# Attention backward loop: every dS unit transposed by DMA, none by TensorE

## The chip, the cores and the metric

The kernel runs on one core of a Trainium2 chip. The metric is the device time of one execution in microseconds (us); lower is better. The kernel before takes 2543.87 us in the median of three runs (2539.78 to 2545.97). Its profile is of one further execution, whose span from the first to the last instruction is 2533.7 us.

## What is computed

The reference is one transformer block with adaptive layer norm, and the gradient of all its inputs. What matters here is attention, `x` of 2048 tokens by 512, 32 heads of 16 columns each, and its backward pass through `jax.vjp`:

```python
qkv = (x @ wqkv).reshape(B, S, 3, H, Dh)          # H = 32 heads, Dh = 16
scores = jnp.einsum('bhqd,bhkd->bhqk', q, k) * Dh ** (-0.5)
p = _softmax(scores, axis=-1)
o = jnp.einsum('bhqk,bhkd->bhqd', p, v)
...
_out, _vjp = jax.vjp(_f, A_x, A_wqkv, A_wo, B_w1, B_b1, B_w2, B_b2, c, w_mod)
_grads = _vjp(grad_out)
```

For each head the backward pass rebuilds the probabilities E = exp(scale * q k), forms dP from the output gradient and v, and multiplies them to dS. Then dK sums dS over queries, dV sums E over queries, and dQ sums dS over keys. dK and dV can take dS and E with queries on the partitions, as they are made; dQ needs dS with keys on the partitions, that is, transposed. All outputs (the block's output and nine gradients) are bf16.

## The kernel before

The kernel is one program with stages: projections and the forward attention (to about 1000 us of the profile), the dense layers and their gradients interleaved with it, the attention backward loop (about 1123 to 2408 us), and a last stage that turns dQ, dK and dV into the gradients of the input and the weights. The change lies in the backward loop alone.

**Units and blocks.** The loop runs over 512 units: 8 head groups of 4 heads, 4 key chunks of 512 keys, 4 query chunks, 4 query tiles of 128 queries. A unit holds 128 queries by 4 heads by 512 keys: 128 partitions of 2048 bf16 elements, 512 KB. Four units with the same head group, key chunk and query chunk form a block; there are 128 blocks.

**What is done for a unit.**

- `score` (line 1595): four TensorE matmuls, one a head, each into one PSUM bank of 128x512. The banks A, B and C are taken in an order that a string gives (`bank`). Bank C has the tag `px`.
- `expo` (line 1601): four ScalarE exponentials from those banks into the SBUF tile `E_u` (4 buffers).
- `dp_pair` (lines 1613 and 1615): for each pair of heads two TensorE matmuls into a PSUM tile `psD_u`, and one VectorE multiplication with `E_u` into the SBUF tile `dS_u` (6 buffers). So a unit has two VectorE instructions.
- `k_quad` and `v_quad` (lines 1650 and 1659): four TensorE matmuls each, summed in the PSUM tile `accVK` over the 16 query tiles, and copied out by ScalarE (line 1662).
- `transpose_unit` (line 1628): the SP queue issues one DMA transpose of the whole `dS_u` into a quarter of the block's tile `dsT` (3 buffers, one a block).

**What is done for a block.** `dq_quad` (line 1677) makes 16 TensorE matmuls from `dsT` into the PSUM tile `dqacc`, also under the tag `px`; `dq_out` (lines 1687, 1690 and 1695) copies it with ScalarE and adds it up on GpSimd.

**The fourth unit of every odd block** is treated otherwise: `transpose_unit` returns without a DMA, and `pe_turn` (line 1640) makes 16 TensorE transposes of 128x128 in two halves, each into a PSUM tile under the tag `px`; ScalarE copies each half into `dsT` (line 1756, 128x1024 elements). That is one unit in eight: 448 units go by DMA, 64 by TensorE. Around the two halves `keep_warm` (line 1633) adds matmuls with a zero weight tile to `accVK`, which change no value; the token f places them.

**What sets the order.** TensorE, ScalarE, VectorE, SP and GpSimd run in the written order in this stage. The order is two token strings: s is a score, e an exponential, D a `dp_pair` (and after every second one the unit's transpose), q a `k_quad` or `v_quad`, t and T a half of `pe_turn` and its ScalarE copy, f a `keep_warm`, d half of a block's `dq_quad`, and Q its `dq_out`. `order_t` serves the passes whose preceding block is odd, `order_n` the others. D runs about one unit behind e, and a pass that issues the scores of block b issues the `dq_quad`s of block b-2:

```python
order_t = ("s0 s1 q s2 e0 e1 D s3 D e2 s4 e3 t1 e4 q T1 D "
    "s5 s6 e5 f f t2 e6 s7 T2 e7 D s8 e8 D f f s9 e9 q q s10 "
    "s11 e10 D d1 d2 e11 Q q s12 D e12 s13 e13 q s14 D e14 "
    "s15 q q e15 ").split(), "ABCABBABACABABCA"
order_n = ("s0 D s1 q e0 q s2 e1 e2 D s3 s4 q s5 e3 D e4 "
    "e5 s6 q s7 D s8 e6 e7 d1 e8 s9 D d2 e9 q Q s10 "
    "s11 e10 D q s12 e11 e12 s13 e13 D q s14 s15 e14 e15 D q ").split(), "CBACBACBABABCABC"
```

**Other transfers in the loop.** ScalarE's queue issues the loads of the next head group and the stores of dK, dV and dQ (lines 1577 and 1667, 1699), from a list of due times in units. SP issues, besides the transposes, five loads for the last stage in the last head group (line 1547) and the last stage's loads after the last transposes (lines 1775 and on).

Of the kernel before, what the change touches and what calls it, by code (L numbers as in the profile page):

```python
# [14 lines left out]
AF = mybir.ActivationFunctionType  # L15
ALU = mybir.AluOpType
AX = mybir.AxisListType
BF = dt.bfloat16
F32 = dt.float32

P = 128
D = 512
# [12 lines left out]
def kernel(  # L35
# [17 lines left out]
    PE = nc.tensor  # L53
    DVE = nc.vector
    ACT = nc.scalar
# [6 lines left out]
    identb = persist.tile([P, P], BF, name="identb")  # L62
# [84 lines left out]
    with ExitStack() as ph:  # L147
# [1053 lines left out]
        def head_fill(i):  # L1201
            for key in ("k", "v", "q", "do"):
                POOL.memset(hsets[i][key][:], 1.0 if key in ("k", "v") else 0.0)
# [345 lines left out]
    with ExitStack() as ph:  # L1549
# [4 lines left out]
        psx = ph.enter_context(tc.tile_pool(name="psIx", bufs=1, space=bass.MemoryType.PSUM))  # L1554
        units = [(hg, kc, qc, qi) for hg in range(HG) for kc in range(QC) for qc in range(QC) for qi in range(4)]
        NU = len(units)
        hst, bst, sst, dqt, cur = {}, {}, {}, {}, {}

        def load_head(hg):
            st = dict(hsets[hg % 2])  # L1560
            st["qz"] = qz[hg % 2]
            st["acc"] = stg.tile([P, n], F32, name="dQacc", tag="dQacc", bufs=1)
            st["dq"] = stg.tile([P, n], BF, name="dQst", tag="dQst", bufs=1)
            st["vk"] = stg.tile([P, n], BF, name="vkb", tag="vkb")
            hst[hg] = st
# [22 lines left out]
        def score(u, hq, bank):  # L1588
            hg, kc, qc, qi = units[u]
            st = hst[hg]  # L1590
            qt = qc * 4 + qi
            r = 32 * hq
            psS = psx.tile([P, 512], F32, name=f"psS_{bank}", tag=banks[bank])
            sst[u, hq] = psS
            PE.matmul(psS[:], st["q"][r:r + 32, qt * P:(qt + 1) * P], st["k"][r:r + 32, kc * 512:kc * 512 + 512],  # L1595
                      start=True, stop=True, tile_position=(r, 0))

        def expo(u, hq):
            if hq == 0:
                bst[u] = [ework.tile([P, 4, 512], BF, name="E_u", tag="E_u"), None]  # L1600
            ACT.activation(bst[u][0][:, hq, :], sst.pop((u, hq))[:], AF.Exp, scale=SCALE)  # L1601

        def dp_pair(u, pair):
            hg, kc, qc, qi = units[u]
            st = hst[hg]
            qt = qc * 4 + qi
            if pair == 0:
                bst[u][1] = ework.tile([P, 4, 512], BF, name="dS_u", tag="dS_u", bufs=6)
            E_u, dS_u = bst[u]
            psD = psd.tile([P, 2, 512], F32, name="psD_u", tag="pd")  # L1610
            for hi in range(2):
                r = 32 * (2 * pair + hi)
                PE.matmul(psD[:, hi, :], st["do"][r:r + 32, qt * P:(qt + 1) * P], st["v"][r:r + 32, kc * 512:kc * 512 + 512],  # L1613
                          start=True, stop=True, tile_position=(r, 0))
            DVE.tensor_tensor(dS_u[:, 2 * pair:2 * pair + 2, :], psD[:], E_u[:, 2 * pair:2 * pair + 2, :], ALU.mult)  # L1615
            if qi == 3 and on_pe(u // 4):
                held["dS"] = dS_u

        def on_pe(b):
            return b % 2 == 1  # L1620

        def transpose_unit(u):
            hg, kc, qc, qi = units[u]
            if qi == 0:
                dqt[u // 4] = tpool.tile([P, 4, 16, P], BF, name="dsT", tag="dsT")
            if qi == 3 and on_pe(u // 4):
                return
            SP.dma_start(out=dqt[u // 4][:, qi], in_=bst[u][1].rearrange("p h k -> p (h k)"), transpose=True)

        held = {}  # L1630

        def keep_warm():
            PE.matmul(cur["vk"][0:DH, :], KS_tok[:, 0, D:QPAD], dOs_tok[:, 0, :], start=False, stop=False,
                      tile_position=(0, 0), skip_group_check=True)

        def pe_turn(b, half):
            pt = psx.tile([P, 8, P], BF, name="ptT", tag="px")
            for i in range(8):
                kt = i % 4
                PE.transpose(pt[:, i, :], held["dS"][:, 2 * half + i // 4, kt * P:(kt + 1) * P], identb[:])  # L1640
            dst = dqt[b][:, 3, 8 * half:8 * half + 8, :]
            held[half] = (dst, pt)

        def k_quad(u):
            hg, kc, qc, qi = units[u]
# [34 lines left out]
        def dq_out(b):  # L1680
# [17 lines left out]
                    r = hg % 2 * 64 + hq * DH  # L1698
                    at(cur["j"] + 6 + hq, load, dQc[hg // 2, r:r + DH, :], st["dq"][32 * hq:32 * hq + DH, :])

        order_t = (
            "s0 s1 q s2 e0 e1 D s3 D e2 s4 e3 t1 e4 q T1 D "
            "s5 s6 e5 f f t2 e6 s7 T2 e7 D s8 e8 D f f s9 e9 q q s10 "
            "s11 e10 D d1 d2 e11 Q q s12 D e12 s13 e13 q s14 D e14 "
            "s15 q q e15 ").split(), "ABCABBABACABABCA"
        order_n = (
            "s0 D s1 q e0 q s2 e1 e2 D s3 s4 q s5 e3 D e4 "
            "e5 s6 q s7 D s8 e6 e7 d1 e8 s9 D d2 e9 q Q s10 "
            "s11 e10 D q s12 e11 e12 s13 e13 D q s14 s15 e14 e15 D q ").split(), "CBACBACBABABCABC"
# [6 lines left out]
        with tc.manual_schedule(engines={PE.engine, ACT.engine, DVE.engine, SP.engine, POOL.engine}):  # L1716
            head_fill(1)
            POOL.memset(qz[1][:], 0.0)
            nD, nq = -1, -4
            idle = psx.tile([P, 512], F32, name="idle", tag="accVK")  # L1720
            for b in range(NU // 4 + 3):
                toks, bank = order_t if on_pe(b - 1) else order_n
                for tok in toks:
                    c, i = tok[0], int(tok[1:] or 0)
                    if c == "s" and b < NU // 4:
                        if i == 0 and units[4 * b][1:] == (0, 2, 0) and units[4 * b][0] + 1 < HG:
                            load_head(units[4 * b][0] + 1)
                        score(4 * b + i // 4, i % 4, bank[i])
                    elif c == "e" and b < NU // 4:
                        expo(4 * b + i // 4, i % 4)  # L1730
                        if b < 2 and i % 2 == 1:
                            if nq > 0:
                                keep_warm()
                            elif nq < 0:
                                PE.matmul(idle[:], ones_bf[:], identb.unsqueeze(1).to_broadcast([P, 4, P]), start=True, stop=True)
                    elif c == "D":
                        if 0 <= nD < 2 * NU:
                            dp_pair(nD // 2, nD % 2)
                            if nD % 2 == 1:
                                transpose_unit(nD // 2)  # L1740
                        nD += 1
                        cur["j"] = nD
                        for j in sorted(j for j in todo if j <= nD):
                            for f, args in todo.pop(j):
                                f(*args)
                    elif c == "q":
                        if 0 <= nq < 2 * NU:
                            (v_quad if nq % 2 else k_quad)(nq // 2)
                        nq += 1
                    elif c == "f" and 0 < nq < 2 * NU:  # L1750
                        keep_warm()
                    elif c == "t" and 0 <= b - 1 < NU // 4:
                        pe_turn(b - 1, i - 1)
                    elif c == "T" and 0 <= b - 1 < NU // 4:
                        dst, pt = held.pop(i - 1)
                        ACT.activation(dst, pt[:], AF.Identity)  # L1756
                    elif c == "d" and 0 <= b - 2 < NU // 4:
                        for kt in (2 * i - 2, 2 * i - 1):
                            dq_quad(b - 2, kt)
                    elif c == "Q" and 0 <= b - 2 < NU // 4:  # L1760
                        dq_out(b - 2)
            assert not todo
        dq_last = hst[HG - 1]["dq"]

    with ExitStack() as ph:
# [15 lines left out]
        order = (("vk", 6), ("vk", 0), ("vk", 1), ("vk", 2), ("vk", 3), ("dq", 0), ("vk", 7), ("dq", 1), ("vk", 4), ("dq", 2), ("vk", 5), ("dq", 3))  # L1781
# [140 lines left out]
        with tc.manual_schedule(engines={PE.engine, ACT.engine, DVE.engine}):  # L1922
            for k, (key, i) in enumerate(order):
                for g in range(2):
                    if (2 * k + g) % 2 == 0:
                        pt = pst.tile([P, 8, P], BF, name="ptq", tag="ptq")
                    else:
                        pt = psd.tile([P, 8, P], BF, name="ptd", tag="pdh1")
                    for ti in range(8):
                        t = 8 * g + ti  # L1930
                        PE.transpose(pt[:, ti, :], xs[key, i][:, t * P:(t + 1) * P], identb[:])
                    if key == "dq":
                        dst = dq_tok[:, 8 * g:8 * g + 8, i * P:(i + 1) * P]
                    else:
                        dst = dvk_tok[:, 8 * g:8 * g + 8, i, :]
# [32 lines left out]
            for b in range(3):  # L1968
                for ic in range(DC):
                    dwqkv(b, ic)  # L1970
                    i = b * DC + ic
# [75 lines left out]
```

## Time and profile before

| | |
|---|---|
| Time, median of 3 runs | 2543.87 us (2539.78 to 2545.97) |
| Span of the profiled execution | 2533.7 us; its own time is not recorded apart from the span. The median of the runs is 10.2 us above it |
| Backward loop, first DMA transpose issued to the SP queue's last one done issuing | 1126.15 to 2405.17 us: 1279.0 us |
| Busy, whole span | TensorE 93%, ScalarE 91%, VectorE 71%, GpSimd 14% |
| Busy, 1400 to 1600 us | TensorE 192.85, VectorE 190.54, ScalarE 197.18 of 200 us |
| Mean granted TensorE clock | 0.978 of full speed |

How to read what follows: a row of a group of instructions gives source line, engine, operation, output and inputs, shapes and count, then the busy time in us and the mean of one in ns, then the idle time of the engine just before these instructions and what ended it. SPq is the SP engine's DMA queue: its rows are the issuing instructions, and their duration is the time for which the queue was held by one, not the transfer itself. A view of the DMA queues gives the packets and bytes that each queue moved in a stretch, and the share of the 16 DMA engines that they took; the share can pass 100%, because packets of one engine overlap in the records.

### The profile page before, as it was taken

To read this page: it belongs to the slowest core of one execution; us is meant where nothing else is said; L and a number is where in the kernel's file an instruction comes from. 1 tells how busy PE (TensorE), PEld (TensorE's weight loads), DVE (VectorE), ACT (ScalarE), POOL (GpSimd) and SP (SyncE) were. 2 spreads that over 40 slices of the span, in tenths; PEclk is the share of its full clock that TensorE was granted. 3 is DMA by queue.
4 is the path that set the end of the run, shared out by engine and by line. 5 is a ranking of instruction groups with operands and counts; after the bars stand their busy time and mean duration, and the time that the engine had idled before them with its cause. 6 is when DMAs were issued, how large, how long until landed. Compare 5 with 4: busy or idle time off the path is not lost.

```text
span 2533.7 us, 50560 instructions
## 1 busy us (share of the span) xinstructions
PE 2353.2 (93%) x19005; PEld 777.5 (31%) x19005; DVE 1808.8 (71%) x2317; ACT 2305.1 (91%) x3577; POOL 348.5 (14%) x370
## 2 busy tenths in 40 slices
PE   7898889989988998999999999999999999999999
PEld 3232223223322323533232223232232322332343
DVE  5555153454444455579899999899998998998872
ACT  7999999999999999549999999999999998998952
POOL 2000001211323141110101101011010110100100
PEclk9999999999999999999899999999999999999999
DMA  6477454366649765979999999999999999999972
GB/s 204 126 191 190 140 130 128 90 164 144 94 101 193 129 144 119 276 199 194 189 201 199 198 197 203 197 195 201 206 202 195 202 195 199 202 203 207 200 241 73
DMA packets 1227131, 447.21 MB, mean 177 GB/s; under 512 B 1103096, under 2 KB 1197752, under 8 KB 1226631
## 3 DMA queue, kind: packets, MB, share of 16 engines
q1 hardware_dynamic: 1198966, 409.14, 81.9%
q0 software_dynamic: 10944, 16.78, 4.6%
q10 hardware_dynamic: 16976, 18.07, 2.6%
q8 instruction: 149, 2.44, 0.4%
q14 instruction: 96, 0.78, 0.1%
HBM read 96.75 MB, written 73.95 MB: 67 GB/s over the span
## 4 chain that ended last, share of the span: by engine, by line
PE 41%; ACT 37%; DVE 7%; issue 7%; DMA 5%; SPq 2%; ACTq 0%; POOL 0%; DVEq 0%; POOLq 0%
ACT E_u L1601 23%; ACT ET L562 11%; PE dqacc L1677 5%; PE psST L560 4%; PE psS_A L1595 3%; PE pm L233 3%; DMA dsT<-dS_u 2%; PE accVK L1650 2%; PE oacc L576 2%; PE psS_B L1595 2%; ACT dsT L1756 2%; PE pdh L1871 2%; PE psS_C L1595 2%; SPq L178 2%; PE pm L412 2%
## 5 line engine op out<-in xcount | busy, mean ns | idle before, releaser
L1615 DVE TENSOR_TENSOR dS_u<-psD_u,E_u 128x1024 bf16<-128x1024 f32 x1024 | 1186.1, 1216 | 93.0 <-PE psD_u L1613 27.2
L562 ACT ACTIVATE ET<-psST 128x1024 bf16<-128x1024 f32 x1024 | 942.7, 1240 | 23.4 <-PE psST L560 22.7
L1601 ACT ACTIVATE E_u<-psS_A 128x512 bf16<-128x512 f32 x768 | 507.8, 661 | 14.1 <-DMA out_dram<-xlast 7.2
L1601 ACT ACTIVATE E_u<-psS_B 128x512 bf16<-128x512 f32 x768 | 501.2, 653 | 8.9 <-PE psD_u L1613 2.2
L1613 PE MATMUL psD_u<-iv,ido 32*128 32x512 bf16 x2048 | 412.0, 390 | 5.4 <-DVE dS_u L1615 5.2
L560 PE MATMUL psST<-qt_sb,kt_sb 32*128 32x512 bf16 x2048 | 315.7, 387 | 50.4 <-ACT ET L562 45.5
L1601 ACT ACTIVATE E_u<-psS_C 128x512 bf16<-128x512 f32 x512 | 332.8, 650 | 13.4 <-DMA dsT<-dS_u 9.9
L1595 PE MATMUL psS_A<-ik,iq 32*128 32x512 bf16 x768 | 296.2, 386 | 11.2 <-ACT E_u L1601 1.1
L1595 PE MATMUL psS_B<-ik,iq 32*128 32x512 bf16 x768 | 297.1, 387 | 9.4 <-ACT E_u L1601 1.9
L1595 PEld LDWEIGHTS <-iq 32*128 32x128 bf16 x2048 | 130.0, 91 | 319.1 <-issue 303.4
L1650 PE MATMUL accVK<-dS_u,qz 128*32 128x512 bf16 x2048 | 215.4, 392 | 0.9 <-DVE dS_u L1615 0.6
L576 PE MATMUL oacc<-ET,vaug 128*32 128x512 bf16 x2048 | 207.4, 395 | 3.2 <-DVE ostage L580 3.2
L1659 PE MATMUL accVK<-E_u,dOs_tok 128*16 128x512 bf16 x2048 | 204.6, 388 | 0.0
L1695 POOL TENSOR_TENSOR dQacc<-dQacc,dqtmp 128x512 f32<-128x512 f32 x64 | 81.3, 1270 | 875.5 <-ACT dqtmp L1690 875.5
L1595 PE MATMUL psS_C<-ik,iq 32*128 32x512 bf16 x512 | 195.1, 381 | 4.2
L560 PEld LDWEIGHTS <-kt_sb 32*128 32x128 bf16 x2048 | 85.1, 91 | 339.6 <-issue 319.1
L1677 PE MATMUL dqacc<-dsT,KS_tok 128*32 128x512 bf16 x2048 | 150.1, 392 | 25.2 <-ACT E_u L1601 10.9
L1756 ACT ACTIVATE dsT<-ptT 128x1024 bf16<-128x1024 bf16 x128 | 144.4, 1128 | 10.1 <-PE ptT L1640 9.6
L251 DVE COPY part<-pm 128x512 f32<-128x512 f32 (+2 forms) x103 | 63.4, 616 | 117.6 <-PE pm L233 109.2
L1613 PEld LDWEIGHTS <-ido 32*128 32x128 bf16 x2048 | 105.8, 91 | 105.7 <-issue 99.5
L1650 PEld LDWEIGHTS <-qz 128*32 128x32 bf16 x2048 | 58.9, 94 | 179.2 <-issue 164.9
L576 PEld LDWEIGHTS <-vaug 128*32 128x32 bf16 x2048 | 53.0, 93 | 122.2 <-issue 122.2
(407 smaller groups left out, 2515.4 us busy)
## 6 DMA issues: line engine op xcount, KB each, us to landing
p_st<-part POOLq DMA_DIRECT2D x36, 256.0 KB, 5.2
kt_sb<-qkT_st SPq DMA_DIRECT2D x124, 64.0 KB
wA<-in_B_w_dram SPq DMA_DIRECT2D x28, 256.0 KB
dsT<-dS_u SPq DMA_TRANSPOSE x448
wB<-w1T_st SPq DMA_DIRECT2D x21, 256.0 KB
wA<-w2T_st SPq DMA_DIRECT2D x21, 256.0 KB
wB<-in_B_w_dram SPq DMA_DIRECT2D x21, 256.0 KB
p_st<-part POOLq DMA_DIRECT2D x25, 192.0 KB, 4.2
```

What stands on the lines that cost most here:

```text
L560: PE.matmul(ps[:, hi, :], kt_sb[r:r + 32, kt * P:(kt + 1) * P], qt_sb[r:r + 32, :], start=True, stop=True, tile_position=(r, 0))
L562: ACT.activation(ET[:, 2 * pair:2 * pair + 2, :], ps[:], AF.Exp, scale=SCALE)
L576: PE.matmul(oacc[32 * hq:32 * hq + 32, :], lhsT, ET[:, hq, :], start=(kt == 0), stop=(kt == TT - 1), tile_position=(0, 32 * hq), skip_grou ...
L1595: PE.matmul(psS[:], st["q"][r:r + 32, qt * P:(qt + 1) * P], st["k"][r:r + 32, kc * 512:kc * 512 + 512], start=True, stop=True, tile_positi ...
L1601: ACT.activation(bst[u][0][:, hq, :], sst.pop((u, hq))[:], AF.Exp, scale=SCALE)
L1613: PE.matmul(psD[:, hi, :], st["do"][r:r + 32, qt * P:(qt + 1) * P], st["v"][r:r + 32, kc * 512:kc * 512 + 512], start=True, stop=True, til ...
L1615: DVE.tensor_tensor(dS_u[:, 2 * pair:2 * pair + 2, :], psD[:], E_u[:, 2 * pair:2 * pair + 2, :], ALU.mult)
L1650: PE.matmul(cur["vk"][32 * hq:32 * hq + 32, :], hst[hg]["qz"][:, qt, hq, :], bst[u][1][:, hq, :], start=(qt == 0), stop=False, tile_positi ...
L1659: PE.matmul(acc[32 * hq:32 * hq + DH, :], dOs_tok[:, qt, (hg * 4 + hq) * DH:(hg * 4 + hq + 1) * DH], E_u[:, hq, :], start=False, stop=(qt ...
L1677: PE.matmul(acc[32 * hq:32 * hq + 32, :], KS_tok[:, kc * 4 + kt, h * DH:h * DH + 32], tT[:, :, hq * 4 + kt, :], start=(kt == 0), stop=(kt ...
L1695: POOL.tensor_tensor(dst2, dst, tmp[:], ALU.add)
L1756: ACT.activation(dst, pt[:], AF.Identity)
```

## The change

All 512 units go through `transpose_unit`. `on_pe`, `held`, `pe_turn`, the ScalarE copies (token T), the tokens t and f and the string `order_t` are gone; every pass runs the string `order_n` with its bank order. `keep_warm` remains in the first two passes only. The order of SP's other transfers, the pools and their buffer counts, and everything outside the loop are as they were.

```diff
             DVE.tensor_tensor(dS_u[:, 2 * pair:2 * pair + 2, :], psD[:], E_u[:, 2 * pair:2 * pair + 2, :], ALU.mult)
-            if qi == 3 and on_pe(u // 4):
-                held["dS"] = dS_u
-
-        def on_pe(b):
-            return b % 2 == 1
 
         def transpose_unit(u):
             hg, kc, qc, qi = units[u]
             if qi == 0:
                 dqt[u // 4] = tpool.tile([P, 4, 16, P], BF, name="dsT", tag="dsT")
-            if qi == 3 and on_pe(u // 4):
-                return
             SP.dma_start(out=dqt[u // 4][:, qi], in_=bst[u][1].rearrange("p h k -> p (h k)"), transpose=True)
...
-        def pe_turn(b, half):
-            pt = psx.tile([P, 8, P], BF, name="ptT", tag="px")
-            for i in range(8):
-                kt = i % 4
-                PE.transpose(pt[:, i, :], held["dS"][:, 2 * half + i // 4, kt * P:(kt + 1) * P], identb[:])
-            dst = dqt[b][:, 3, 8 * half:8 * half + 8, :]
-            held[half] = (dst, pt)
...
-        order_t = (
...
-        order_n = (
+        order = (
             "s0 D s1 q e0 q s2 e1 e2 D s3 s4 q s5 e3 D e4 "
             "e5 s6 q s7 D s8 e6 e7 d1 e8 s9 D d2 e9 q Q s10 "
             "s11 e10 D q s12 e11 e12 s13 e13 D q s14 s15 e14 e15 D q ").split(), "CBACBACBABABCABC"
...
-                toks, bank = order_t if on_pe(b - 1) else order_n
+                toks, bank = order
...
-                    elif c == "f" and 0 < nq < 2 * NU:
-                        keep_warm()
-                    elif c == "t" and 0 <= b - 1 < NU // 4:
-                        pe_turn(b - 1, i - 1)
-                    elif c == "T" and 0 <= b - 1 < NU // 4:
-                        dst, pt = held.pop(i - 1)
-                        ACT.activation(dst, pt[:], AF.Identity)
```

## The prediction

> **What bounds the kernel now.** First the page's busy shares: over the loop TensorE, ScalarE and VectorE are all above 90%, so none of them singles itself out. Then the slices of the DMA engines, where the loop begins at about slice 18:
>
> ```profile
> DMA  6477454366649765979999999999999999999972
> GB/s 204 126 191 190 140 130 128 90 164 144 94 101 193 129 144 119 276 199 194 189 201 199 198 197 203 197 195 201 206 202 195 202 195 199 202 203 207 200 241 73
> ```
>
> The reader is to see that the DMA row is at 9 through the whole loop, and that the rate there hardly moves, 189 to 207 GB/s, which is how a limit looks. A busy share alone does not prove one, so next the time-ordered rows of the SP queue, then the transposes' own row:
>
> ```profile
> 1126.15 1137.26 SPq L1628 DMA_TRANSPOSE dsT<-dS_u  x399
> 2263.46 0.99 SPq L1547 DMA_DIRECT2D iq<-dVKtP  x1
> 2264.55 9.31 SPq L1628 DMA_TRANSPOSE dsT<-dS_u  x3
> ```
>
> ```profile
> L1628 SPq DMA_TRANSPOSE dsT<-dS_u x448: 1681/2670/4379, 1126.1 to 2401.7; - x150
> ```
>
> 399 transposes are issued one behind the other, shown as one piece: 1137.26 / 399 = 2.85 us each. The shortest issue took 1.681 us, so the usual 2.67 is not what issuing must cost; the queue is held by what lies before it. The view of SP's waits between 1150 and 2430 us (total, times, longest) names another cause:
>
> ```profile
> SPq L1628 <- DVE dS_u L1615: 946.0, 439, 4.3
> ```
>
> This says VectorE, and I do not believe it, because dS is there long before. I counted both lines up to one unit (two windows, to 1709.1 and to 1701.4 us):
>
> ```profile
> L1628 SPq DMA_TRANSPOSE dsT<-dS_u x203: 1681/2682/4379, 1126.1 to 1709.0; - x102
> ...
> L1615 DVE TENSOR_TENSOR dS_u<-psD_u,E_u x462: 1210/1214/1226, 1124.9 to 1701.3; 128x1024 bf16<-128x1024 f32 x154
> ```
>
> 462 VectorE instructions are units 0 to 230. Of these 231 units 28 are the fourth of an odd block, so 203 have a DMA transpose. The last of them begins to issue at 1709.0, though its data was done at 1701.3 + 1.2 = 1702.5: 6.5 us late, two to three transposes. The queue works off a backlog. So the loop sits on two limits at once: the engines make 4 units in 1279.0 / 128 = 9.99 us, and the DMA turns 3.5 of them in that time.
>
> **What one transpose costs the DMA.** I looked for stretches in which nothing but transposes moved, and for one with other traffic (12.3, 12.0 and 21 us long, from 1281.1, 2317.9 and 1699 us):
>
> ```profile
> DMA packets 10349, 2.61 MB, mean 212 GB/s; under 512 B 10349, under 2 KB 10349, under 8 KB 10349
> ```
>
> ```profile
> DMA packets 10381, 2.62 MB, mean 218 GB/s; under 512 B 10381, under 2 KB 10381, under 8 KB 10381
> ```
>
> ```profile
> q1 hardware_dynamic: 14556, 3.67, 119.6%
> q10 hardware_dynamic: 128, 0.26, 3.9%
> ```
>
> A unit is 0.524 MB. The quiet stretches give 0.524 / 212 GB/s = 2.47 us and 2.40 us; a third, 1744.6 to 1752.2 us at 208 GB/s, gives 2.52. I take the middle, 2.47. In the third stretch above, SP's queue (q1) moved 3.67 MB, 7 units, in 21 us: 3.0 us each, while ScalarE's queue (q10) moved only 0.26 MB. So the loads of the next head cost the transposes more than their bytes. Over the loop 448 x 2.47 = 1106.6 us are bare transposes; 1279.0 - 1106.6 = 172.4 us are other transfers, what they cost the transposes, and the few gaps.
>
> **The change, part by part.**
>
> *Added: 64 DMA transposes*, on a queue that has no room. 64 x 2.47 = **+158.1 us**. The 172.4 us stay, since the other transfers are the same in number and size. The engines give nothing back: a block then needs (512 x 2.47 + 172.4) / 128 = 11.2 us of the queue, against 9.99 us that the engines need today. Bounds: from below, the other transfers might cost no more than their own share of the DMA engines in the loop (4.3% for ScalarE's queue, 0.5% for instructions and the rest, of 1279.0 us: 61 us) and some 14 us for the five or six 512 KB loads on SP; then 512 x 2.47 + 75 = 1340 us, +61. From above, each added transpose meets traffic as the present ones do: 64 x 2.85 = +182. I take +158, which is nearer to the row that counts this kernel's own transposes in bulk.
>
> *Removed: 128 ScalarE copies* (144.4 us busy, 1128 ns each) and *1024 TensorE transposes* (82.3 us busy), 255 of the 266 zero products (84.7 us busy, overlapping others). They lie on ScalarE and TensorE, which after the change wait for the queue, so they are worth 0. If the queue were faster than I think, they are worth up to what VectorE leaves: its 1024 instructions come one each 1.146 us where nothing stops them (10 in 11.46 us at 1811.66), 1174 us, and 93.0 us idle before them, so at most 93 us.
>
> *Moved: every pass uses the string of the even ones.* It ends with s15 in bank C and begins with s0 in bank C, where before the two strings alternated and the borders differed (C then A, A then C). So at each of 127 borders s0 waits for e15 (0.65 us), and ScalarE then waits for s0 (0.38 us); behind s0 on TensorE are D and the q matmuls, so VectorE waits too. 0.4 to 1.0 us a border, 50 to 130 us in all if nothing covered it. The cover is the queue's 11.2 us a block against the engines' 9.99 less the removed copies (144.4 / 128 = 1.1 us a block): some 2 us. I cost it at 0.
>
> *Moved by the backlog: where the engines stop.* Up to 6 units of dS may be held (6 buffers), and d1 in a pass needs the transposes of two blocks before, while about 6 younger units are already made. So TensorE stops at line 1677 and VectorE at line 1615 with 5 or 6 units queued, some 13 us of work: the queue does not run dry while they restart. These stops cost no more than the queue's own time, as long as the restart is shorter than that. The chain of waits (start, length, what) has such stops already:
>
> ```profile
> 1622.62 6.85 DMA dsT<-dS_u
> 1629.49 0.31 ACTq L1577
> ```
>
> After this one TensorE ran at a granted clock of 0.50 from 1630.2 to 1633.6 us, and the 16 matmuls of line 1677 took 1.90 us instead of twice 0.61. So each long stop brings 3.4 us at half speed, about 1.7 us lost, inside the 13 us of backlog.
>
> *The end of the loop.* The last transpose is now unit 511's, and the stage behind it starts from the queue's end as before: 2533.7 - 2405.2 = 128.5 us, unchanged.
>
> **Sum.** 1126.15 + 512 x 2.47 + 172.4 + 128.5 = 2691.7 us of span, 158.0 more than 2533.7. With the 10.2 us by which the median of the runs exceeds the span, **2702 us**.
>
> [...]
>
> **Rivals.**
>
> 1. *Proportional*: 2.85 us for each added transpose, 2543.9 + 182 = 2726. For it: the 399 in one piece. Against: the other transfers do not grow. It lies within my range.
> 2. *The traffic thins out*: with a queue that is never empty the other transfers hide between the transposes; +61, 2605. Against it: the queue is backlogged today, and still takes 3.0 us with traffic.
> 3. *Restarts not covered*: the stops come every block instead of now and then, each with half speed behind it and the bank border on top; if 0.5 us a block shows, 64 us more: 2766. It decides where TensorE at half speed needs longer than the backlog lasts.
> 4. *Faster*: the transposes run at the pace of the freed engines. It needs all traffic together in under 1279 / 512 = 2.50 us a unit; beyond that point the 144.4 us of copies come off ScalarE and VectorE's 93 us of idle time bound the gain. Half of it, 46 us: 2498. For it: quiet stretches do reach 2.40 to 2.52, just at the point. Against: the queue's mean is 2.85 with nothing idle between.
> 5. *No change*: the queue absorbs 64 more, and the freed engine time is lost at the bank borders: 2544. It needs both 4's condition and the border price.
>
> **Chances.** Forecast with rival 1, 2640 to 2750: 0.80. Rival 2 below 2640: 0.07. Rival 3 above 2750: 0.07. Rival 4: 0.04. Rival 5: 0.02. The range is 2640 to 2750; the low end goes towards rival 2, and the high end lies between rivals 1 and 3. A measurement of this kernel tells about 0.3%, 8 us, from no change: faster 0.04, same 0.02, slower 0.94.
>
> **What would show it.** The profile after has 512 transposes in a stretch of about 1437 us, 2.8 us each, with the DMA row at 9; ScalarE's and VectorE's busy shares in the loop fall to some 80 to 85%; lines 1677 and 1615 now wait for `dsT<-dS_u` for 100 us and more in sum; quiet stretches still show 208 to 218 GB/s. I am wrong if the transposes take under 2.5 us in the mean, if SP's queue shows gaps, or if the waits at s0 of a block carry the chain.

## The result, and the profile after

The changed kernel takes 2692.06 us (median of four runs, 2687.72 to 2694.22), the kernel before 2541.82 us in its four runs. The ratio is **1.0596, 95% interval 1.057 to 1.0621**: 150 us slower. The prediction was 2702 us with a range of 2640 to 2750. The span of the profiled execution is 2685.9 us.

The page's slices of the kernel after, in the place of those shown of before (PEclk is the granted TensorE clock in tenths):

```profile
PEclk9999999999999999878888788787886887878789
DMA  7476562468476669799999999999999999999982
GB/s 204 130 188 166 146 148 78 130 166 141 89 154 146 132 122 273 193 183 202 197 201 199 208 202 201 205 202 199 199 202 203 207 204 198 200 208 206 198 246 83
```

The DMA row is at 9 through the loop and the rate is where it was, about 200 GB/s. The loop is longer because more bytes pass at the same rate. What is new is the clock row. It was at 9 in all but one slice of before, and is now at 6 to 8.

The SP queue in order of time, and the transposes' row:

```profile
1126.23 1271.97 SPq L1621 DMA_TRANSPOSE dsT<-dS_u  x455
2398.25 0.58 SPq L1547 DMA_DIRECT2D iq<-dVKtP  x1
```

```profile
L1621 SPq DMA_TRANSPOSE dsT<-dS_u x512: 1619/2558/4433, 1126.2 to 2556.5; - x171
```

455 transposes stand in one piece of 1271.97 us, 2.80 us each (before: 399 at 2.85). One piece is no proof of a backlog, here or in the prediction, because the view merges rows of one kind across waits. A run below (e7), whose queue waits for the engines, shows its transposes as one piece too, 5.08 us each:

```profile
1133.18 1159.29 SPq L1623 DMA_TRANSPOSE dsT<-dS_u  x228
```

What tells a backlog is how long a finished dS waits, which follows below. The queue is done issuing the last one at 2558.41 us, 1432.2 us after the first (before: 1279.0). What follows takes 2685.9 - 2558.4 = 127.5 us (before: 128.5). The loop grew by 153.2 us and the span by 152.2, so all of the loss lies in the loop.

This is the same count as in the prediction, of transposes issued and VectorE instructions begun (windows from 1126 us to 1858.6 and to 1849 us). One VectorE instruction lies before the window in both kernels, so one is to be added to its count:

```profile
L1621 SPq DMA_TRANSPOSE dsT<-dS_u x261: 1619/2524/4094, 1126.2 to 1858.6; - x131
```

```profile
L1615 DVE TENSOR_TENSOR dS_u<-psD_u,E_u x521: 1214/1217/1226, 1124.9 to 1848.4; 128x1024 bf16<-128x1024 f32 x174
```

521 + 1 halves are units 0 to 260, the last done at 1848.4 + 1.2 = 1849.6 us. Its transpose, the 261st, begins to issue 9.0 us later. I left out that one instruction in the prediction, so the lag that I gave for before, 6.5 us, was 7.6. Over the whole loop a finished dS waits 3.0 us (median) for its transpose's issue before, and 6.3 us after. Only 25 of 448 transposes before and 21 of 512 after begin within 0.1 us of their data, so the queue was behind nearly all the time in both kernels.

The engines between 1400 and 2200 us, before and after (busy time of TensorE, its weight loads, VectorE, ScalarE and GpSimd, then the clock, the DMA share and GB/s):

```profile
1400.00:2200.00 800.00, 760.39 (x7260) 237.44 (x7257) 747.35 (x646) 773.51 (x1474) 91.18 (x66) 0.99 1.17 199
```

```profile
1400.00:2200.00 800.00, 688.69 (x5803) 164.81 (x5795) 679.41 (x580) 650.09 (x1250) 83.13 (x61) 0.81 1.17 203
```

VectorE fell from 93% to 85%, ScalarE from 97% to 81%; the DMA's numbers hardly moved. The waits of the loop (total, times, longest) show where the stops are:

```profile
DVE dS_u L1615 <- PE psD_u L1613: 130.4, 174, 5.4
PE psS_C L1595 <- ACT E_u L1601: 102.0, 119, 2.4
...
ACT E_u L1601 <- DMA dsT<-dS_u: 42.3, 19, 6.1
...
DVE dS_u L1615 <- DMA dsT<-dS_u: 22.3, 23, 2.1
```

The second line is the bank border (s0 waits for e15). It looks large, and whether it costs anything no wait row can say. Nor do the direct waits for the transposes account for the loss: 42.3 and 22.3, and 9.9 us at line 1660 (5.0 of its matmuls and 4.9 of their weight loads). The 42.3 us are ScalarE's, whose exponentials read no transposed data. Each of these 19 waits stands just behind a DMA issue of ScalarE's own (line 1577), which was held until one of SP's transposes had landed; ScalarE runs in the written order, so its exponentials stood still with it. A stop of one engine shows up as the other engines' waits for that one: TensorE at line 1660 waited for ScalarE 43 times, 40.9 us. In the chain that ended last, the transposes' share of the loop went from 4.8% to 11.7%.

### The profile page after: what moved, and what is told of

Same layout as the page of the kernel before. It is cut to its first block, busy times and chain, and to the rows that moved or that the text cites. A ratio compares the mean times of both kernels' runs of the same rounds, so it can differ in the third digit from the quotient of the medians.

```text
span 2685.9 us, 48010 instructions
## 1 busy us (share of the span) xinstructions
PE 2368.4 (88%) x17724; PEld 695.9 (26%) x17724; DVE 1825.4 (68%) x2317; ACT 2223.3 (83%) x3449; POOL 347.2 (13%) x370
## 4 chain that ended last, share of the span: by engine, by line
PE 50%; ACT 26%; DMA 8%; DVE 8%; issue 6%; SPq 1%; ACTq 0%; POOL 0%; DVEq 0%
ACT E_u L1601 14%; ACT ET L562 11%; DMA dsT<-dS_u 6%; PE dqacc L1660 6%; PE psS_A L1595 5%; PE psS_B L1595 4%; PE psS_C L1595 4%; PE accVK L1633 4%; PE accVK L1642 3%; PE psST L560 3%; PE pm L233 2%; PE oacc L576 2%; DVE dS_u L1615 2%; PE pdh L1842 2%; PE pwq L1876 2%
## 5 line engine op out<-in xcount | busy, mean ns | idle before, releaser
L1601 ACT ACTIVATE E_u<-psS_B 128x512 bf16<-128x512 f32 x768 | 468.5, 610 | 112.2 <-PE psD_u L1613 69.2
L1613 PE MATMUL psD_u<-iv,ido 32*128 32x512 bf16 x2048 | 467.0, 452 | 10.5 <-DVE dS_u L1615 10.2
L1601 ACT ACTIVATE E_u<-psS_C 128x512 bf16<-128x512 f32 x640 | 392.7, 614 | 98.9 <-PE psS_B L1595 59.8
L1601 ACT ACTIVATE E_u<-psS_A 128x512 bf16<-128x512 f32 x640 | 393.6, 615 | 43.2 <-PE psD_u L1613 20.1
L1595 PE MATMUL psS_B<-ik,iq 32*128 32x512 bf16 x768 | 347.0, 452 | 23.6 <-ACT E_u L1601 14.1
L1595 PE MATMUL psS_C<-ik,iq 32*128 32x512 bf16 x640 | 276.3, 432 | 103.5 <-ACT E_u L1601 102.0
L1660 PE MATMUL dqacc<-dsT,KS_tok 128*32 128x512 bf16 x2048 | 207.9, 492 | 61.7 <-ACT E_u L1601 40.9
L1633 PE MATMUL accVK<-dS_u,qz 128*32 128x512 bf16 x2048 | 245.8, 461 | 2.2 <-DVE dS_u L1615 1.7
L1642 PEld LDWEIGHTS <-dOs_tok 128*16 128x16 bf16 x2048 | 49.7, 87 | 152.0 <-issue 152.0
L1660 PEld LDWEIGHTS <-KS_tok 128*32 128x32 bf16 x2048 | 41.1, 100 | 182.1 <-issue 168.4
```

Of the source, the lines that this page charges most:

```text
L1633: PE.matmul(cur["vk"][32 * hq:32 * hq + 32, :], hst[hg]["qz"][:, qt, hq, :], bst[u][1][:, hq, :], start=(qt == 0), stop=False, tile_positi ...
L1642: PE.matmul(acc[32 * hq:32 * hq + DH, :], dOs_tok[:, qt, (hg * 4 + hq) * DH:(hg * 4 + hq + 1) * DH], E_u[:, hq, :], start=False, stop=(qt ...
L1660: PE.matmul(acc[32 * hq:32 * hq + 32, :], KS_tok[:, kc * 4 + kt, h * DH:h * DH + 32], tT[:, :, hq * 4 + kt, :], start=(kt == 0), stop=(kt ...
```

## The experiments

**Theories.** *Queue*: the SP transpose queue sets the loop's end, before nearly and after wholly. *Border*: s0 waits for e15 at 127 borders. *Clock*: TensorE at half speed, since the zero products and the turns are gone, is what is late.

The ratio is to the kernel before. The clock is that of 1400 to 2200 us, and the last column is the median time for which a finished dS waits for its transpose's issue (by the trace, unit by unit).

| Run | DMA transposes | Ratio (95%) | Clock | dS waits, us |
|---|---|---|---|---|
| before | 448 | 1 | 0.99 | 3.0 |
| after | 512 | 1.0596 (1.057 to 1.0621) | 0.81 | 6.3 |
| e1_only_add | 512 | 1.0628 (1.0585 to 1.0672) | 0.88 | 6.9 |
| e2_only_order | 448 | 1.0107 (1.0056 to 1.0158) | 0.87 | 1.6 |
| e3_other_banks | 512 | 1.0616 (1.0583 to 1.065) | 0.83 | 7.3 |
| e4_no_v_products | 512 | 1.0827 (1.079 to 1.0864) | 0.54 | 0.03 |
| e5_no_head_loads | 512 | 1.0468 (1.0438 to 1.0499) | 0.81 | 6.7 |
| e6_one_in_sixteen | 480 | 1.0322 (1.0288 to 1.0355) | 0.89 | 4.9 |
| e7_half_the_transposes | 256 | 1.0036 (1.0013 to 1.0058) | 0.87 | 0.03 |
| e8_v_for_zero | 512 | 1.0559 (1.0531 to 1.0586) | 0.81 | 6.6 |
| e9_zero_products | 512 | 1.0642 (1.0604 to 1.0679) | 0.94 | 5.2 |
| e10_half_banks_zero | 256 | 1.0212 (1.018 to 1.0243) | 1.00 | 0.03 |
| e11_half_banks | 256 | 0.9626 (0.9594 to 0.9657) | 1.00 | 0.03 |
| e12_before_no_zero | 448 | 1.0089 (1.0067 to 1.0112) | 0.94 | 2.0 |

### The 64 transposes alone, and the order alone

In the kernel before, `transpose_unit` no longer returns early, and the copies of the TensorE turns go to a tile that is not read:

```diff
-            if qi == 3 and on_pe(u // 4):
-                return
...
-            dst = dqt[b][:, 3, 8 * half:8 * half + 8, :]
+            dst = wk.tile([P, 8, P], BF, name="unread", tag="unread", bufs=2)[:]
```

> The kernel before, with both token strings, the TensorE turns, the ScalarE copies and the zero products all kept; only the 64 left-out DMA transposes are added, and ScalarE's copies go to a tile that nothing reads. Queue theory (SP's transpose queue sets the loop's end): as the changed kernel, 2685 to 2710 us, 512 transposes at 2.80 us. Clock theory (the loss comes from TensorE at half speed once the zero products and the fixed rhythm are gone): under 2600, since they are all there. Border theory (s0 waits for e15 at 127 block borders): 2545, since the old strings have no such border.

The run takes 1.0628, 2705 us. With every turn, copy and zero product still there, the added transposes bring the whole loss. The SP queue of this run:

```profile
1136.41 1281.87 SPq L1626 DMA_TRANSPOSE dsT<-dS_u  x455
```

That is 2.82 us each. The other half of the change is the changed kernel without those 64 (its three `dsT` tiles are allocated once and set to zero, so that an unwritten quarter may stay; dQ is then wrong):

```diff
+            if qi == 3 and u // 4 % 2 == 1:
+                return
             SP.dma_start(out=dqt[u // 4][:, qi], in_=bst[u][1].rearrange("p h k -> p (h k)"), transpose=True)
```

> The changed kernel without the fourth unit's transpose in odd blocks (that quarter of dsT keeps old data, so dQ is not computed rightly): 448 transposes, one token string, no TensorE turns. Queue theory: 448 x 2.47 + 172 = 1279 us of loop, 2530 to 2555. Border theory: the price of 127 borders stays, 2590 to 2670. Clock theory: 2600 and more.

The run takes 1.0107, 2570 us. Border and clock expected 2590 and more, the queue theory at most 2555; it lies between, so no theory alone met it. The order has a price of some 27 us where the queue is less loaded (a dS waits 1.6 us). The two prices do not add up: 6.28% and 1.07% apart, 5.96% together.

> The kernel before with TensorE turning the fourth unit of every fourth block only: 480 transposes by DMA, 32 units by TensorE, the old string t around those and the other string elsewhere. Queue theory: half of the 64 added transposes, so about half of the loss: 1.030 of before, 2610 to 2630. Border or clock theories: the runs above gave the order at most 1.011 by itself, so under 1.012.

In the kernel before only `on_pe` changes, from `b % 2 == 1` to `b % 4 == 1`. The run takes 1.0322, 2627 us: 448, 480 and 512 transposes give 1, 1.032 and 1.060.

### The bank border

```diff
-            "s11 e10 D q s12 e11 e12 s13 e13 D q s14 s15 e14 e15 D q ").split(), "CBACBACBABABCABC"
+            "s11 e10 D q s12 e11 e12 s13 e13 D q s14 s15 e14 e15 D q ").split(), "CBACBACBABABACBA"
```

> The changed kernel with another bank order, whose last score uses bank A and not C, so that s0 of the next block waits for nothing. Queue theory: 2692 within 8 us; the waits of bank C at line 1595 (102 us in the changed kernel) go, and come back at lines 1660 and 1615. Border theory: 40 us or more off.

The run takes 1.0616, no gain. The 102 us of TensorE at bank C are gone from the waits. TensorE's waits at the banks A and B and the waits for the transposes have grown in their place (bank B from 14.1 us, bank A from next to none):

```profile
ACT E_u L1601 <- DMA dsT<-dS_u: 57.8, 22, 5.3
DVE dS_u L1615 <- ACT E_u L1601: 50.4, 65, 4.6
...
DVE dS_u L1615 <- DMA dsT<-dS_u: 43.7, 49, 2.1
...
PE psS_B L1595 <- ACT E_u L1601: 35.8, 28, 4.7
PE psS_A L1595 <- ACT E_u L1601: 30.6, 87, 0.4
```

So a wait of 102 us in the table was worth nothing, because the queue was later. It is worth a great deal where the queue is not. The next three runs leave out the transposes of every second unit, so their dQ is wrong; the second has the banks of the diff above as well, and the third those and the string with six zero products that is shown further down:

```diff
+            if qi % 2 == 1:
+                return
```

> The changed kernel with the transposes of every second unit left out (those quarters of dsT keep old data, so dQ is not computed rightly): 256 transposes need some 256 x 2.47 + 172 = 805 us, far under the engines' pace. It shows what the engines need under the new order when the queue never holds them. If the queue alone had set the loop before and after: 2450 to 2500. If the order without turns and zero products has a price of its own, as the run with 448 transposes hints (1.0107 of before): 2550 to 2580, TensorE's clock at 0.85 to 0.9 in the loop.

> The same with the other bank order and no zero products: tells the two apart. If the border waits (98 us at line 1595 with 448 transposes) were what the order cost: below 2510, as with both. If it was TensorE's clock: near 2554, and only the zero products help.

> The run with half of the transposes, with the bank order that has no wait at the block border and six zero products a pass. With a free queue, 1.0036 of before was what the engines needed under the new order, though 144 us of ScalarE's copies were gone. If the border and the half-speed stretches took that gain: 40 us or more under before, below 2500. If the engines' pace has another bound (VectorE, 1174 us at its closest): still within 20 us of before.

With half of the transposes the new order takes 2554 us, as long as before, though 144 us of ScalarE's copies and 82 us of TensorE's turns are gone. With the other banks it takes 2449.5. The border cost 104 us, 0.8 us for each of 127. TensorE's time at half speed in the loop went with it, from 382 us to 48, so the 104 us are the border's waits and the slow clock behind them together; no run parts the two. Without the border VectorE is busy 99% of the time, and the clock stays at 1.00 without a zero product in this stretch:

```profile
1400.00:2200.00 800.00, 723.53 (x6991) 202.37 (x6988) 793.41 (x700) 780.64 (x1509) 97.61 (x72) 1.00 0.72 130
```

That is the pace of the engines with a queue that never holds them and no turns: 96 us under before. Six zero products a pass on top make it 2599.5, outside both expectations (below 2500, or within 20 us of before). 768 of them cost 150 us, 0.195 us each, since TensorE is then the late one (790.64 of 800 us busy).

### TensorE's clock

> The changed kernel without the 2048 TensorE products of E and the output gradient (line 1642), so dV is not computed. A fifth of TensorE's work in the loop is gone, and no transfer. Queue theory: 2692 within 10 us. Clock theory (TensorE, half of the time at half speed, is what is late): 50 us or more off.

The edit takes out the four matmuls in `v_quad` and lets those of `k_quad` close the sum, so dV is not computed. The run takes 1.0827, 2754 us, **some 60 us slower than after, for less work**. Neither expectation foresaw that: I had looked for no change or a gain. The row for 1400 to 2200 us:

```profile
1400.00:2200.00 800.00, 685.02 (x4387) 135.27 (x4384) 649.20 (x548) 626.90 (x1180) 77.93 (x57) 0.54 1.08 192
```

The clock is at 0.54: half speed for 1362 us of the run's loop, against 555 us after and 71 us before (from the first transpose's issue to the end of the last one's). And a finished dS waits only 0.03 us (median; 363 of 512 begin within 0.1 us), so the queue mostly waits for the engines. The DMA share is 1.08 all the same, so a DMA row at 9 does not prove a backlog either. Here the clock theory holds, and the queue theory does not. One zero product in place of each four V products:

```diff
-            for hq in range(4):
-                PE.matmul(acc[32 * hq:32 * hq + DH, :], dOs_tok[:, qt, (hg * 4 + hq) * DH:(hg * 4 + hq + 1) * DH], E_u[:, hq, :],
-                          start=False, stop=(qt == TT - 1), tile_position=(0, 32 * hq), skip_group_check=True)
+            keep_warm()
```

> The changed kernel with each four V products replaced by one zero product (line 1633's form), so dV is not computed. Without V products the loop took 1.0827 of before with the clock at 0.55 and an idle queue. If that loss was the clock, and one zero product keeps TensorE as busy as the four products side by side: back to the queue's limit, 2685 to 2710, clock 0.8. If the loss was something else that the V products did: still 2750.

The run takes 1.0559, 2690 us: back at the queue's limit, with the clock at 0.81.

```profile
1400.00:2200.00 800.00, 689.86 (x4949) 162.83 (x4941) 683.80 (x584) 653.39 (x1257) 83.09 (x61) 0.81 1.16 203
```

TensorE's busy time is hardly different between the last two rows (685 and 690 us), because its matmuls are longer at half speed (685.02 us for 4387 of them is 156 ns each, 689.86 us for 4949 is 139; a score matmul of before took 0.37 us at 1624.49 us, at a clock of 1.00, and 0.60 us at 1632.75 us, at 0.50); the busy column does not show this, the clock column does. Is the changed kernel itself held by its clock of 0.81? Its string with six zero products:

```diff
-            "s0 D s1 q e0 q s2 e1 e2 D s3 s4 q s5 e3 D e4 "
-            "e5 s6 q s7 D s8 e6 e7 d1 e8 s9 D d2 e9 q Q s10 "
-            "s11 e10 D q s12 e11 e12 s13 e13 D q s14 s15 e14 e15 D q ").split(), "CBACBACBABABCABC"
+            "s0 D s1 q f e0 q s2 e1 e2 D s3 s4 q s5 f e3 D e4 "
+            "e5 s6 q s7 D s8 f e6 e7 d1 e8 s9 D d2 e9 q Q s10 f "
+            "s11 e10 D q s12 e11 e12 s13 f e13 D q s14 s15 f e14 e15 D q ").split(), "CBACBACBABABCABC"
```

> The changed kernel with six zero products a pass put back into the string. Queue theory: the clock rises from 0.81 to 0.9 or more in the loop, and the time stays at 2692 within 10 us. If the half-speed stretches cost time of their own in the changed kernel: 20 us or more off.

The clock rises from 0.81 to 0.94, and the time to 1.0642. The faster clock bought nothing here; the time lies 12 us (by the ratios) to 17 us (by the medians) above after, a little more than the 10 that I had allowed. The zero products are work for TensorE too, so this run is not the clock alone; but a finished dS still waits 5.2 us for the queue. So after is the queue's, not the clock's.

The stop that the prediction showed left TensorE idle for 3.71 us, with a clock of 0.50 behind it. Stops of that length are too few to account for the slow clock: after has 60 half-speed stretches in the loop, and TensorE stood idle for more than 3.71 us three times; without the V products there are 40 stretches, 1362 us in all, and the longest idle time is 1.8 us. So much shorter stops went with the slow clock here. The border's are among them, as 382 us of half speed with it against 48 without show in the pair above; under the full queue the other bank order leaves 533 us of after's 555, and no run shows what the clock went with there.

### The head's loads

```diff
-            for i, (to, fro) in enumerate(loads):
+            for i, (to, fro) in enumerate(loads if hg == 1 else ()):
```

> The changed kernel, but the loads of the next head group's k, q, v, do and q rows are issued once only (heads 2 to 7 reuse what is there, so their gradients are of other heads): 126 of ScalarE's transfers in the loop are left out, about 8 of its 14.4 MB. If the loads cost the transposes more than their bytes (172.4 us for all, some 120 of it not gaps): 60 to 90 us off the changed kernel, near 2610 to 2630. If they cost only their own share of the DMA engines (61 us in all): about 35 off, 2655 to 2665. If TensorE's clock and not the queue is what is late: no gain.

132 transfers are left out (22 for each of six heads, 8.07 of 14.40 MB; the expectation says 126), and the gradients are of other heads. The run takes 1.0468, 2669 us: 23 us under after by the medians, 1.3% of before (33 us) by the ratios. The queue's longest piece:

```profile
1133.05 1243.96 SPq L1621 DMA_TRANSPOSE dsT<-dS_u  x455
```

That is 2.73 us each in place of 2.80, 28 us for 455. It is the lower of the two figures expected, about the loads' own share of the DMA engines. So these loads are a small part of what lifts the queue's mean from 2.47 to 2.80. Another part the after trace shows in one transpose (1664.06 to 1667.63 us, 40 slices of 89 ns):

```profile
DMA  9999299900000000000100003999999999999999
GB/s 267 235 166 103 40 350 272 155 0 0 0 0 0 0 0 6 6 9 9 11 6 11 11 9 66 298 284 284 301 287 284 290 298 278 295 295 281 295 295 251
...
q1 hardware_dynamic: 2082, 0.52, 127.0%
q8 instruction: 1, 0.02, 1.6%
```

One 16 KB packet of the queue that the view calls instruction (q8), in what follows an instruction fetch, begins at 1664.54 us and takes 0.93 us. The transpose stream stops for some 1.4 us, and then catches up at 290 GB/s. The transpose needed 3.57 us. So it is nearly everywhere in the loop: 76 of its 81 such packets have a pause of 1.0 us or more in the stream within 2 us of them (under 20 packets of SP's queue begin in each 0.1 us, where the mean is 74), and only 7 such pauses lie elsewhere.

The 511 times from one transpose's issue to the next part as follows. In 81 a fetch packet begins, and they last 3.40 us in the mean; 221 hold no packet of another queue and last 2.48; the other 209 hold packets of ScalarE's queue (loads and stores) or of the second instruction queue (q14) and last 2.90. Above 2.48 that is 74 us for the fetches and 88 us for the rest. No run here took the fetches away, so this is a reading and not an experiment, and it may be too high: without the 132 loads the same reading gives 48 us for the rest, 40 less, while the loop became only 25.3 us shorter (1406.9 us).

### The zero products of before

```diff
-        "s5 s6 e5 f f t2 e6 s7 T2 e7 D s8 e8 D f f s9 e9 q q s10 "
+        "s5 s6 e5 t2 e6 s7 T2 e7 D s8 e8 D s9 e9 q q s10 "
```

> The kernel before with its zero products (token f) taken out and nothing else: one part of the change alone. 448 transposes stay, and there is no bank border to wait at. The run with six zero products a pass showed one to cost TensorE some 0.2 us when it is what is late, 255 of them 50 us; the queue, with 448 transposes at the 2.80 us of the changed kernel, needs 1254 us instead of the 1279 of before. If the engines were the later of the two in the kernel before: 10 to 25 us faster, 2520 to 2535. If the zero products kept the clock up at TensorE's waits: 2560 and more. If the queue set the pace alone: no change within 8 us.

The run takes 1.0089 (1.0067 to 1.0112), 2562 us. I hoped for a version faster than before and got one 0.9% slower. Without its zero products the kernel before drops from a clock of 0.99 to 0.94, and a finished dS waits 2.0 us for the queue and not 3.0: the engines fall behind it. The 256 zero products were worth 22 us there, as the second of the three expectations had it.

## Why the prediction was right, point by point

- **What bounds the kernel: right.** A finished dS waits 6.3 us for the queue, 64 more transposes alone give the whole loss (e1), half of them half of it (e6). Of the signs that I named, the single piece of transposes and the DMA row at 9 prove less than I thought (e7 and e4 show them with a queue that waits).
- **The sum: right, 10 us too high.** I foretold 1437 us of loop, and 1432.2 were measured; the end took 127.5 us against 128.5; the median of the runs lies 6.2 us above the span, where before's then known median lay 10.2 above. The 64 added transposes cost 153.2 us of loop, 2.39 us each against the 2.47 of the sum.
- **2.47 us for a transpose in quiet: right.** In the quietest stretch of the trace after, 1646.8 to 1664.1 us, 3.69 MB pass at 213 GB/s: 0.524 / 213 gives 2.46.
- **The 172.4 us beside it: right in size, wrong in what it is.** 1432.2 - 512 x 2.47 leaves 167.6 us. I put it down mainly to the loads of the next head. 132 of those transfers were worth 23 to 33 us (e5). Instruction fetches, which I did not count, take up to some 74 us by the packets. That the size held is in part luck: the loop has 91 fetch packets before and 81 after, so the other transfers were not quite the same in number.
- **Removed work worth 0: right.** "Up to 93 us" with a free queue needed the bank border gone as well: 2554 with it, 2449.5 without, which is 96 us under before.
- **The border at 0, 50 to 130 us if uncovered: right at both ends.** It was worth 0 under the queue (e3) and 104 us with the queue free (e11 against e7). The range was counted from the waits alone, and the 104 us have TensorE's half speed in them, so the size is in part luck.
- **The stops: misread, and too small in number.** I showed the stop of 6.85 us as one of TensorE at line 1677. It was ScalarE's, held at a DMA issue of its own until a transpose had landed, and TensorE waited for ScalarE (kernel before; the first two rows are ScalarE's, the third is TensorE's):

```profile
1629.49 0.31 ACTq L1577 DMA_DIRECT2D dQc<-dQst  x1
1629.84 0.60 ACT L1601 ACTIVATE E_u<-psS_C 128x512 bf16<-128x512 f32 x1 [3.51 <-DMA dsT<-dS_u]
1630.49 1.90 PE L1677 MATMUL dqacc<-dsT,KS_tok 128*32 128x512 bf16 x16 [3.71 <-ACT E_u L1601]
```

  I expected half speed for 3.4 us after long stops. It was 555 us of 1432, in 60 stretches, and only three of TensorE's stops were longer than the 3.71 us of the one above. The backlog covered it, as e9 shows by raising the clock for nothing. But rival 3 was nearer than its 0.07: without the V products the engines did fall behind (e4).
- **Waits of 100 us and more for `dsT<-dS_u`: wrong.** At the two lines that I named 32.2 us (22.3 + 9.9) stand directly against the transposes, 74.5 us with ScalarE's 42.3; the rest shows as engines waiting for one another. VectorE at 85% and ScalarE at 81% were as foretold.
- **Rival 4, faster: its condition failed** (2.80 us a unit against 2.50). In bytes, the loop's mean is 0.524 MB / 2.80 us = 187 GB/s.

What stays open: why kernels with 512 transposes differ by 0.8% among themselves. Their ratios rise with the clock (0.81 at 1.0559, 0.94 at 1.0642), as if a busier TensorE slowed the transposes; nothing here tells that apart from chance in the order. Open too is what the instruction fetches cost, which no run took away. No version tried that computes all outputs beats the kernel before (e11 does, with half of the transposes left out).

## What to carry to other kernels

Before work is moved from an engine to a queue, count how far the queue is behind: compare the time at which a unit's data is done with the time at which its transfer begins. Here a queue that was behind nearly all the time charged 64 added transposes 153 us, 2.39 us each, and removed work, removed waits and a better clock elsewhere were worth nothing, however large their rows were. Test such rows in a run with the queue made light, as the bank border shows: 0 us under the queue, 104 us without it.

## What the runs showed of the hardware

- Less TensorE work cost time here: taking out the V products put the clock at 0.54, from 0.81, and made the kernel some 60 us longer, though TensorE was never idle for more than 1.8 us; one zero product for each four of them brought it back to 0.81 and 2690 us.
- Zero products gained 22 us in the kernel before (256 of them), cost 12 to 17 us under the full queue (768), and cost 150 us, 0.195 us each, where TensorE is the late one (768).
- Beside one 16 KB packet of the instruction queue (0.93 us) the DMA transposes stood still for some 1.4 us, and 76 of the 81 such packets in the loop after have a pause of 1.0 us or more by them. This is read from the trace, and no run took those packets away.
- In the loop after, ScalarE's exponentials stood still 19 times, 42.3 us in all, behind a DMA issue of ScalarE's own that by the trace was held until a transpose of SP's queue had landed.
